# Five small edits to the order of work in a convolution and feed-forward kernel on one core

## The chip, the core and the metric

The kernel runs on one core of one Trainium2 chip. The core has a matrix engine (PE, with PEld for its weight loads), three engines for elementwise work (DVE, ACT, POOL), a queue engine (SP), and 16 DMA engines that move data between HBM and the on-chip memories. The matrix engine writes to PSUM, eight banks of 512 fp32 values per partition; everything else here lives in SBUF. The metric is device time in microseconds of one execution, and lower is better. Engines wait for each other through semaphores, and each engine works through its own instructions in the order in which the program issues them. The order is written by hand in this kernel: nothing reorders it.

## What is computed

Two layers run one after the other on x of shape 8 x 4224 x 192. The first is a causal convolution of 7 taps, with one softmax-normalised set of taps per head (8 heads of 24 channels). The second normalises each row and adds a feed-forward layer of width 768. Cut to the parts that matter:

```
out = np.einsum('hk,bskhg->bshg', softmax(weight), x_unf)       # y, the convolution
xn = (y - mean(y)) / np.sqrt(var(y) + 1e-06) * g_ln
return y + np.maximum(xn @ w_ch1, 0.0) @ w_ch2
```

All of it is fp32. The weight arrays arrive as 64-bit floats and are turned into fp32 on the chip by integer arithmetic (`split_words`, `join_low`, `join_sign`, `join_product`).

## The kernel before, in words

**Groups.** The 33,792 rows are split into 18 groups, numbered g = 0 to 17. Group 0 has 6 rows per partition, group 1 has the 8 rows per partition that are left over at the end of each of the eight sequences, group 2 has 10, and groups 3 to 17 have 16 each. For one group the work is: load x (`load_x`), convolve it into y (`first_tap` and `second_tap` on ACT, `conv` on DVE), transpose y in blocks of 32 into yt (`transpose`, DVE), multiply by the first weight (`up` or `up_mixed`), relu, multiply by the second weight (`down` or `down_fast`), transpose back (`finish_fast`), scale by the row's 1/std (`scale`, ACT) and add to the output that `store_y` has written, with an accumulating DMA (`add_to_out`, issued by POOL).

**The two big stages.** From group 3 on, both products use a recursive scheme with 7 block products in place of 8. It needs sums of quarters of the left side and of the weights. For the first product `sums_of_y` makes them, s1 = a21 + a22 and s2 = s1 - a11 on DVE and s3, s4 on POOL. `up_mixed(g)` runs seven block products over one third of the width (lines 691 to 709) and seven over the rest (712 to 761), all through `rows_of_tiles` (the matmuls are on line 533). Between them ACT copies PSUM away (line 662), DVE adds PSUM to SBUF (line 668) and POOL issues DMAs that add one SBUF tile to another (line 617). `down_fast(g)` runs the seven block products of the second weight (lines 888 to 891, 905, 906 and 909; the matmuls are on line 861). The middle ones read tiles that DVE makes with nine `half_sum` instructions (lines 897 to 899, recorded on line 828).

**What DVE does in `down_fast(g)`**, in its order: the end of the convolution of group g+1, `transpose(g + 1)` (line 893), the nine half sums, three additions to c11 (line 901), s1 and s2 of group g+1 (lines 608 and 609), a memset of one value per partition (line 612) that POOL waits for before s3, and the statistics of group g+1 (`moments`, line 448). After that come, in the next `up_mixed`, `finish_fast` (lines 923 and 925) and the convolution of group g+2 (line 417).

**What ACT does in `down_fast(g)`.** The block products copy their results with ACT (line 867), one copy for each of three chunks. Behind each copy ACT takes some items from a list, `work`, as many as `behind` says: 3 after each chunk of the first product, then 2, 2 and 3, and 2 in lines 905 and 906. The list is put together at the end of `up_mixed` (lines 790 to 793): a relu of `one.c22`, then 14 scalings of the previous group's output (the item of row 7 and the last one also issue an output DMA on POOL), and among them, behind nine items, the two relus of `two.c22` (lines 792 and 675). Then follow the 16 items of `first_tap` and `second_tap` of group g+2; the last of them issues four DMAs on POOL that add tap 1 to y (`add_second_tap`, line 409).

**The start.** PE first runs idle matmuls on no data of interest (`keep_warm`, line 367). DVE and ACT turn the first weight into fp32 in three pieces, and PE then subtracts its mean (`centre_w1`, lines 332 to 348) with matmuls on lines 335 and 340. Between those PE runs the convolution of three heads of group 0 (`conv_on_pe`, line 326); ACT copies those results into y (line 330). The other five heads of group 0 are DVE's. Then `transpose(0)` (line 1000) makes yt of group 0 in one instruction, and `up(0)` starts. Its matmuls read the six blocks of 32 channels in order, and with them six blocks of w1, the last two of which ACT copies at the very end (line 362).

**Loads.** `load_x(1)` (line 994) issues eight DMAs, one for each sequence, all on SP's queue, behind the load of the second weight into `raw2` (line 990). Where `gate` is set, a memset of one value by DVE in front of the DMA makes the DMA wait until DVE has come to that point.

Of the kernel before, what the change touches and what calls it, by code (L numbers as in the profile page):

```python
# [16 lines left out]
def kernel(  # L17
# [29 lines left out]
    nc = tc.nc  # L47
    PSUM = bass.MemoryType.PSUM
    B, S, D = x.shape
    H, K = weight.shape  # L50
    F = moe_w_ch1.shape[1]
    P = 128
# [9 lines left out]
    NC = D // C  # L62
# [23 lines left out]
    CH = NC // 2  # L86
# [46 lines left out]
    def load_x(g, queue=nc.sync, pad=True, gate=False):  # L133
        b, j0, n = groups[g]
        t = xpool.tile([P, J + PAD, D], F32, tag="xg", name=f"xg{g}")
        xg[g] = t
        flat = t.rearrange("p j d -> p (j d)")
        if gate:
            nc.vector.memset(t[0:1, 0:1, 0:1], 0.0)
        if b is None:  # L140
            for b in range(B):
                queue.dma_start(
                    out=flat[LP * b : LP * b + LP, 0 : (PAD + n) * D],
                    in_=bass.AP(
                        tensor=x.tensor, offset=(b * S + P * R - PAD) * D,
                        ap=[[n * D, LP], [1, (PAD + n) * D]],
                    ),
                )
            return
        if j0:  # L150
            queue.dma_start(
                out=flat[:, 0 : (n + PAD) * D], in_=xr[b, :, (j0 - PAD) * D : (j0 + n) * D]
            )
            return
        if b:

            queue.dma_start(
                out=flat[:, 0 : (PAD + n) * D],
                in_=bass.AP(
                    tensor=x.tensor, offset=(b * S - PAD) * D, ap=[[R * D, P], [1, (PAD + n) * D]]  # L160
                ),
            )
            if pad:
                nc.gpsimd.memset(t[0:1, 0:PAD, :], 0.0)
            return
        nc.gpsimd.memset(t[0:1, 0:PAD, :], 0.0)
        for p0, p1 in ((16, P), (1, 16)):
            nc.sync.dma_start(
                out=flat[p0:p1, 0 : (PAD + n) * D],
                in_=bass.AP(  # L170
                    tensor=x.tensor, offset=(b * S + p0 * R - PAD) * D,
                    ap=[[R * D, p1 - p0], [1, (PAD + n) * D]],
                ),
            )
        nc.sync.dma_start(out=flat[0:1, PAD * D : (PAD + n) * D], in_=xr[b, 0:1, 0 : n * D])
# [156 lines left out]
    def centre_w1():  # L332
        pm = [take_bank()[:, 0:FH] for r in range(2)]
        for r in range(2):
            nc.tensor.matmul(pm[r], share[0], w1f[:, r, :], start=True, stop=False)
            if r == 0:
                keep_warm(2)
        conv_on_pe(PE_HEADS[2])
        for r in range(2):
            nc.tensor.matmul(pm[r], share[1 + r], w1f[:, 2, :], start=False, stop=True)  # L340
        tap_matrices(PE_HEADS[1], range(3))
        for r in range(2):
            nc.scalar.copy(mean[:, FH * r : FH * r + FH], pm[r])
        tap_matrices(PE_HEADS[1], range(3, K))
        conv_on_pe(PE_HEADS[0])
        copies_of_w1(0, [(q, 0) for q in range(NQ)])
        conv_on_pe(PE_HEADS[1])
        copies_of_w1(2, [(NQ, 0), (NQ + 1, 0), (NQ, 1), (NQ + 1, 1)])
# [15 lines left out]
    def keep_warm(times):  # L364

        for _ in range(times):
            nc.tensor.matmul(idle[:, 0:P], less, less, start=True, stop=True)
# [224 lines left out]
    ysums, rows_left = {}, {}  # L592
# [5 lines left out]
            cuts = [(slice(0, J), slice(T * h, T * h + T)) for h in range(2)]  # L598
        return [yt[g][:, js, CH * k : CH * k + CH, ts] for js, ts in cuts for k in range(2)]

    def sums_of_y(g, engine):

        room = upool.tile([P, 3 * HJ * CH * C], F32, tag="ys", name=f"ysums{g}")
        room = room.rearrange("p (v j c t) -> p v j c t", v=3, c=CH, t=width(g))
        s1, s2, s3 = [room[:, v] for v in range(3)]
        a11, a12, a21, a22 = quarters_of_y(g)
        ysums[g] = s1, s2, s3, a21
        nc.vector.tensor_tensor(s1, a21, a22, op=ALU.add)
        nc.vector.tensor_tensor(s2, s1, a11, op=ALU.subtract)
        if engine is not nc.vector:  # L610

            nc.vector.memset(s3[:, 0:1, 0:1, 0:1], 0.0)
        engine.tensor_tensor(s3, a21, a11, op=ALU.subtract)
        engine.tensor_tensor(a21, a12, s2, op=ALU.subtract)
# [4 lines left out]
    def up_mixed(g, ahead, pending):  # L619
# [7 lines left out]
        a11, a12, a21, a22 = quarters_of_y(g)  # L627
        s1, s2, s3, s4 = ysums[g]
# [161 lines left out]
        work = [lambda: one.relu(one.c22)]  # L790
        work += [lambda j=j: scale_one(j) for j in range(2, done)]
        half = [lambda i=i: two.relu(two.c22[:, i : i + 1]) for i in range(PAIR)]
        return work[0:9] + half + work[9:]

    def down_row(rows, left):

# [47 lines left out]
    def down_fast(g, work):  # L844
        n = fast[g]
        t = width(g)
        w = n * T
        a = of_products(g)
        flat = cpool.tile([P, NC, NFAST * C], F32, tag="cs", name=f"cs{g}")[:, :, 0 : n * C]
        order = "p c (h j t) -> p c h j t" if t == C else "p c (j h t) -> p c h j t"  # L850
        cs = flat.rearrange(order, h=2, t=t)
        free = a[:, 1, 0].rearrange("p f q j t -> p (f q) j t")
        parts = [free[:, 0:CH], free[:, CH : 2 * CH]]
        banks = [take_bank() for c in range(CH) for i in range(2)]

        def product(bank, left, right, to, first, behind=0):
            for c in range(CH):
                dst = banks[2 * c + bank]
                for f in (PAIR, *range(PAIR)):
                    for q in range(NQ):  # L860
                        nc.tensor.matmul(  # L861
                            dst[C * q : C * q + C, 0:w], right[:, f, C * c : C * c + C],
                            left[:, f, q], start=(first and f == PAIR), stop=(f == PAIR - 1),
                            skip_group_check=True,
                        )
                if to is not None:
                    nc.scalar.copy(  # L867
                        to[:, c], dst[:, 0:w].rearrange("p (j t) -> p j t", t=t)
                    )
                for one in work[:behind]:  # L870
                    one()
                del work[:behind]

        b = quarters_of_w2()
        c11, c21 = cs[:, 0:CH, 0], cs[:, 0:CH, 1]
        c12, c22 = cs[:, CH:NC, 0], cs[:, CH:NC, 1]
        if g == 2:
            work += [lambda h=h: first_tap(4, heads=(h, h + 1)) for h in range(7, H)]
            work += [lambda h=h: second_tap(4, heads=(h, h + 1)) for h in range(H)]
        elif g + 2 < NG:  # L880
            work += [
                lambda tap=tap, h=h: tap(g + 2, heads=(h, h + 1))
                for tap in (first_tap, second_tap) for h in range(H)
            ]
        behind = (1, 1, 1, 1) if g == 2 else (3, 2, 2, 3)
        if g + 1 == NG:
            behind = (0, 0, 1, 2)
        product(0, a[:, 0, 0], b[0], c11, True, behind[0])
        product(1, a[:, 1, 0], w2sums[:, 2], c22, True, behind[1])
        product(1, a[:, 1, 1], w2sums[:, 3], c21, False, behind[2])  # L890
        product(1, a[:, 0, 1], b[2], None, True, behind[3])
        if g + 1 < NG:
            transpose(g + 1)
            if g == 2:
                b11, b12 = quarters_of_w1()[0:2]
                nc.vector.tensor_tensor(b12, b12, b11, op=ALU.subtract)
        half_sum(g, (1, 1), (1, 1), (1, 0), ALU.add)
        half_sum(g, (0, 0), (1, 1), (0, 0), ALU.add)
        half_sum(g, (0, 1), (0, 1), (1, 1), ALU.subtract)
        for c in range(CH):  # L900
            nc.vector.tensor_tensor(
                c11[:, c], c11[:, c], banks[2 * c + 1][:, 0:w].rearrange("p (j t) -> p j t", t=t),
                op=ALU.add,
            )
        product(0, a[:, 1, 1], w2sums[:, 1], parts[0], False, 2)
        product(0, a[:, 0, 0], w2sums[:, 0], parts[1], False, 2)
        for one in work:
            one()
        product(0, a[:, 0, 1], b[3], c12, False)
        if g + 1 < NG:  # L910
            sums_of_y(g + 1, nc.gpsimd)
            if g == 2:
                load_x(5, gate=True)
            moments(g + 1)
        else:
            finish_fast(g, 0, flat, cs, parts)
        return flat, cs, parts
# [73 lines left out]
        out=raw2.rearrange("p (c d) w -> p c (d w)", d=D),  # L991
        in_=w2_words.rearrange("(c p) d -> p c d", p=P),
    )
    load_x(1)
    tap_matrices(PE_HEADS[0], range(4))
    first_tap(0, heads=(0, PE_HEADS[0]))
    tap_matrices(PE_HEADS[0], range(4, K))
    conv(0, heads=(0, PE_HEADS[0]))
    centre_w1()
    transpose(0)  # L1000
    spare = cpool.tile([P, NC * NFAST * C], I32, tag="cs", name="spare")
    words_2 = (raw2, spare[:, 0 : NF * D], spare[:, NF * D : 2 * NF * D])
    split_words(*words_2, scaled=False)
# [13 lines left out]
    for g in range(NG):  # L1017
# [6 lines left out]
        else:  # L1024
            up(g)
            work = []
# [90 lines left out]
```

## Time and profile before

| | |
|---|---|
| device time, median of 3 runs | 953.44 us (951.1 to 954.62) |
| the profiled execution's own time | 953.63 us |
| span of its profile | 951.4 us |
| granted PE clock over the span | 0.999 |
| PE busy / weight loads | 944.5 us / 750.8 us |
| DVE / ACT / POOL busy | 894.1 / 700.0 / 340.8 us |

The span runs from the first to the last instruction of the profile; 2.2 us of the execution's own time lie around it. A group of instructions is named by engine, line and operation, with the tiles it writes and reads (out<-in). In the timeline the columns are start and duration in us, engine, line, operation, tiles, shapes and count; brackets hold the idle time just before and what ended it. PE's durations are modelled and overlap, so in the dense stages the time from one start to the next says more than the busy share. "issue" is idle time for which the profile shows no reason.

### The profile page before, as it was taken

How to read it: one execution, taken by the hardware profiler on the slowest of the kernel's cores; microseconds unless marked ns; L12 is line 12 of the kernel's file. 1: busy time of each engine (PE TensorE's matmuls, PEld its weight loads, DVE VectorE, ACT ScalarE, POOL GpSimd, SP SyncE). 2: the span in 40 equal slices, each digit the busy share in tenths (PEclk: the TensorE clock that was granted, in tenths of full speed). 3: DMA queues.
4: the chain of work that ended last, by engine and by line, in shares of the span. 5: the costliest groups of instructions: out<-in, count | busy, mean ns of one | idle time of the engine just before them, and what ended most of it. 6: DMA issues, size and time to landing. Idle time of an engine off the chain costs nothing.

```text
span 951.4 us, 38106 instructions
## 1 busy us (share of the span) xinstructions
PE 944.5 (99%) x16914; PEld 750.8 (79%) x16914; DVE 894.1 (94%) x1496; ACT 700.0 (74%) x1250; POOL 340.8 (36%) x474
## 2 busy tenths in 40 slices
PE   9999999999999999999999999999999999999998
PEld 7998896877859687787968778696877869586787
DVE  7999998999999999999999999999999999999867
ACT  6853678597877959787895968779696877967362
POOL 1158422723144142534218231452416332261330
PEclk9999999999999999999999999999999999999999
DMA  8359589689797887979697897979889797778261
GB/s 207 102 159 209 100 222 285 123 181 245 136 259 146 233 172 171 234 136 272 132 246 148 192 227 134 272 134 250 163 188 219 129 278 136 174 134 144 40 121 68
DMA packets 39834, 169.37 MB, mean 178 GB/s; under 512 B 4469, under 2 KB 8182, under 8 KB 33655
## 3 DMA queue, kind: packets, MB, share of 16 engines
q0 software_dynamic: 32864, 106.77, 60.5%
q1 hardware_dynamic: 6800, 60.16, 17.2%
q8 instruction: 133, 2.18, 0.9%
q14 instruction: 31, 0.25, 0.1%
q10 hardware_dynamic: 6, 0.00, 0.0%
HBM read 38.93 MB, written 50.33 MB: 94 GB/s over the span
## 4 chain that ended last, share of the span: by engine, by line
PE 67%; DVE 0%; issue 0%
PE ps L861 34%; PE ps L533 32%; PE ps L798 1%; DVE y L955 0%
## 5 line engine op out<-in xcount | busy, mean ns | idle before, releaser
L417 DVE SCALAR_TENSOR_TENSOR y<-xg,taps,y 128x384 f32<-128x384 f32 (+3 forms) x720 | 364.7, 582 | 3.3 <-DMA y<-tb 1.7
L861 PE MATMUL ps<-room,w2sums 128*32 128x256 f32 (+2 forms) x4608 | 246.9, 371 | 0.0
L533 PE MATMUL ps<-yt,w 32*128 32x256 f32 (+2 forms) x4160 | 237.9, 373 | 0.3 <-DVE yt L428 0.3
L533 PEld LDWEIGHTS ps<-yt,w 32*128 32x128 f32 x4160 | 211.0, 185 | 21.6 <-issue 6.2
L861 PEld LDWEIGHTS ps<-room,w2sums 128*32 128x32 f32 x4608 | 151.4, 110 | 89.5 <-ACT room L675 4.6
L662 ACT COPY room<-ps 128x512 f32<-128x512 f32 (+1 forms) x213 | 174.2, 859 | 62.6 <-PE ps L533 62.6
L861 PE MATMUL ps<-room,w 128*32 128x256 f32 (+2 forms) x3456 | 189.9, 371 | 0.4 <-DVE room L668 0.3
L828 DVE TENSOR_TENSOR room<-room 128x1024 f32<-128x1024 f32 (+2 forms) x147 | 161.2, 1170 | 22.4 <-PE ps L861 14.9
L861 PEld LDWEIGHTS ps<-room,w 128*32 128x32 f32 x3456 | 112.9, 110 | 69.3 <-DVE room L668 5.3
L533 PE MATMUL ps<-ysums,w1sums 32*128 32x256 f32 x2160 | 127.2, 376 | 0.3 <-issue 0.3
L533 PEld LDWEIGHTS ps<-ysums,w1sums 32*128 32x128 f32 x2160 | 116.5, 185 | 5.3 <-issue 0.7
L951 POOL DMA_DIRECT2D out_dram<-ot x69 | 59.0, 941 | 155.4 <-ACT ot L940 102.3
L409 POOL DMA_DIRECT2D y<-tb x59 | 52.5, 1386 | 154.5 <-ACT room L867 110.2
L867 ACT COPY cs<-ps 128x256 f32<-128x256 f32 (+2 forms) x192 | 70.0, 367 | 45.8 <-PE ps L861 45.8
L675 ACT ACTIVATE room<-room 128x1024 f32<-128x1024 f32 (+1 forms) x89 | 92.8, 1072 | 3.2 <-DMA room<-parts_cs 3.2
L940 ACT ACTIVATE ot<-ot,r 128x192 f32<-128x192 f32 x224 | 90.9, 464 | 0.0
L380 ACT ACTIVATE y<-xg,taps 128x384 f32<-128x384 f32 (+3 forms) x141 | 73.1, 608 | 0.4 <-DMA xg<-in_x_dram 0.4
L448 DVE BATCH_NORM_STATS2 st<-y 128x6 f32<-128x192 f32 x264 | 70.1, 344 | 0.0
L867 ACT COPY room<-ps 128x256 f32<-128x256 f32 (+2 forms) x96 | 35.5, 370 | 46.6 <-PE ps L861 44.9
L533 PE MATMUL ps<-yt,w1sums 32*128 32x256 f32 x1080 | 69.2, 375 | 0.0
L533 PE MATMUL ps<-ysums,w 32*128 32x256 f32 x1080 | 68.5, 374 | 0.0
L398 ACT ACTIVATE tb<-xg,taps 128x384 f32<-128x384 f32 (+1 forms) x120 | 66.1, 628 | 0.0
(119 smaller groups left out, 939.9 us busy)
## 6 DMA issues: line engine op xcount, KB each, us to landing
xg<-in_x_dram SPq DMA_DIRECT2D x14, 2112.0 KB, 16.2
room<-room POOLq DMA_DIRECT2D x45, 512.0 KB, 5.3
out_dram<-ot POOLq DMA_DIRECT2D x59, 384.0 KB, 9.6
y<-tb POOLq DMA_DIRECT2D x58, 384.0 KB, 8.8
out_dram<-y SPq DMA_DIRECT2D x13, 1536.0 KB, 9.1
room<-parts_cs POOLq DMA_DIRECT2D x28, 512.0 KB, 6.8
room<-parts_tb POOLq DMA_DIRECT2D x14, 1024.0 KB, 7.6
xg<-in_x_dram POOLq DMA_DIRECT2D x1, 2112.0 KB, 14.0
```

Of the source, the lines that this page charges most:

```text
L380: nc.scalar.mul(y[g][:, 0:n, cs], xg[g][:, 0:n, cs], taps[:, h, 0:1])
L398: nc.scalar.mul(tb[g][:, 0:n, cs], xg[g][:, 1 : 1 + n, cs], taps[:, h, 1:2])
L417: nc.vector.scalar_tensor_tensor(out=y[g][:, 0:n, cs], in0=t[:, k : k + n, cs], scalar=taps[:, h, k : k + 1], in1=y[g][:, 0:n, cs], op0=AL ...
L448: nc.vector.bn_stats(out=sums[g][:, j, :], in_=y[g][:, j, :])
L533: nc.tensor.matmul(banks[:, q, i * w + j1 * t : i * w + j2 * t], right[rows, c, P * i : P * i + P], left[rows, j1:j2, c, :], start=start, ...
L662: nc.scalar.activation(to, of, AF.Relu) if relu else nc.scalar.copy(to, of)
L675: nc.scalar.activation(c, c, AF.Relu)
L828: nc.vector.tensor_tensor(a[:, *dst, f], a[:, *left, f], a[:, *right, f], op=op)
L861: nc.tensor.matmul(dst[C * q : C * q + C, 0:w], right[:, f, C * c : C * c + C], left[:, f, q], start=(first and f == PAIR), stop=(f == PAI ...
L867: nc.scalar.copy(to[:, c], dst[:, 0:w].rearrange("p (j t) -> p j t", t=t))
L940: nc.scalar.mul(ots[g][:, j, :], ots[g][:, j, :], rstd[g][:, j : j + 1])
L951: nc.gpsimd.dma_start(out=rows[:, d0:d1], in_=src[:, d0:d1], accum_op=ALU.add)
```

## The change

1. `load_x(1)` is gated, with the memset over all 128 partitions, and its last four DMAs are issued by POOL (`nc.gpsimd`) and not by SP.
2. The two idle matmuls inside `centre_w1` are removed.
3. The sum s1 of group g+1 is made in a function of its own, right behind `transpose(g + 1)`, ahead of the nine half sums. s2, s3 and s4 stay where they were.
4. In the work list the two relus of `two.c22` come behind seven items and not nine, and an item that does nothing stands between them. With 3 items behind each chunk of the first product, the first relu and the empty item end the first product's share, and the second relu is the first item of the second product's share.
5. `transpose(0)` is issued as two instructions, over the first and the last three blocks of channels.

```diff
         if gate:
-            nc.vector.memset(t[0:1, 0:1, 0:1], 0.0)
+            nc.vector.memset(t[0 : 1 if b is not None else P, 0:1, 0:1], 0.0)
         if b is None:
             for b in range(B):
-                queue.dma_start(
+                (queue if b < B // 2 else nc.gpsimd).dma_start(
                     out=flat[LP * b : LP * b + LP, 0 : (PAD + n) * D],
...
             nc.tensor.matmul(pm[r], share[0], w1f[:, r, :], start=True, stop=False)
-            if r == 0:
-                keep_warm(2)
         conv_on_pe(PE_HEADS[2])
...
-    def sums_of_y(g, engine):
-
+    def first_sum_of_y(g):
         room = upool.tile([P, 3 * HJ * CH * C], F32, tag="ys", name=f"ysums{g}")
         room = room.rearrange("p (v j c t) -> p v j c t", v=3, c=CH, t=width(g))
         s1, s2, s3 = [room[:, v] for v in range(3)]
         a11, a12, a21, a22 = quarters_of_y(g)
         ysums[g] = s1, s2, s3, a21
         nc.vector.tensor_tensor(s1, a21, a22, op=ALU.add)
+
+    def sums_of_y(g, engine):
+        a11, a12, a21, a22 = quarters_of_y(g)
+        s1, s2, s3, _ = ysums[g]
         nc.vector.tensor_tensor(s2, s1, a11, op=ALU.subtract)
...
-        return work[0:9] + half + work[9:]
+        return work[0:7] + [half[0], lambda: None, half[1]] + work[7:]
...
             transpose(g + 1)
+            first_sum_of_y(g + 1)
             if g == 2:
...
-    load_x(1)
+    load_x(1, gate=True)
...
-    transpose(0)
+    transpose(0, 0, CH)
+    transpose(0, CH, NC)
```

## The prediction, made before the changed kernel was run

> **What bounds the kernel.** I read the page's busy shares and the chain that ended last, then the windows of single `down_fast` stages, then who waited for whom, then the timeline around each edit.
>
> ```profile
> PE 944.5 (99%) x16914; PEld 750.8 (79%) x16914; DVE 894.1 (94%) x1496; ACT 700.0 (74%) x1250; POOL 340.8 (36%) x474
> PE ps L861 34%; PE ps L533 32%; PE ps L798 1%; DVE y L955 0%
> ```
>
> PE is busy all along and alone makes the chain from 312.6 us to the end. The pieces of that chain are nearly constant: 27.6 us for an `up_mixed`, 27.4 for a `down_fast`. So work taken from DVE, ACT or a queue is worth nothing by itself; only a stall of PE, or work that PE does itself, can be won. PE's busy time hides short stalls, so I compared whole stages. These are the windows of two `down_fast` (the columns are the window, its length, then the busy times, the clock, the DMA share and GB/s):
>
> ```profile
> 312.63:339.96 27.33, 27.33 (x504) 16.32 (x504) 26.25 (x38) 22.52 (x51) 9.35 (x10) 1.00 0.96 245
> 367.58:395.00 27.42, 27.42 (x507) 16.17 (x505) 26.23 (x38) 22.72 (x51) 9.35 (x10) 1.00 0.96 247
> ```
>
> They do the same work, and the second is 0.09 us longer. The waits of PE's weight loads in these two windows show why: the second has a wait of 0.4 us for ACT's relu on L675, and the first has none. Over the run:
>
> ```profile
> PEld ps L861 <- ACT room L675: 4.6, 13, 0.4
> PE ps L861 <- DVE room L668: 0.3, 1, 0.3
> ```
>
> **The relus (edit 4).** The third block product of `down_fast` reads the relued c22. ACT's timeline, in the group whose stage starts at 422.61, shows the relus late:
>
> ```profile
> 427.70 0.37 ACT L867 COPY cs<-ps 128x256 f32<-128x256 f32 x1
> 427.96 1.16 ACT L940 ACTIVATE ot<-ot,r 128x192 f32<-128x192 f32 x3
> 429.01 0.37 ACT L867 COPY cs<-ps 128x256 f32<-128x256 f32 x1
> 429.26 2.02 ACT L675 ACTIVATE room<-room 128x1024 f32<-128x1024 f32 x2
> 431.16 0.37 ACT L867 COPY cs<-ps 128x256 f32<-128x256 f32 x1
> ```
>
> ACT works without a pause here. A scaling takes it (429.01 - 427.96)/3 = 0.35 us, a copy 0.26 from start to start, a relu 0.96. Product three starts when two products of 3.9 us are over, at 430.4. Its first 8 of 24 matmuls per chunk read `one.c22`, the next 8 the first relu's block, and the third 8 the second relu's, at 430.4 + 16 x 0.053 = 431.28. The second relu ends at 431.28: just too late. After the change ACT does copy 427.70, one scaling at 427.96, the first relu at 428.31, the copy at 429.27, the second relu at 429.53, ending at about 430.6. That is 0.7 us sooner, so this wait goes. The copy at 429.01 moves to 429.27 and ends at 429.64; it frees the bank that product three writes from 430.4 on, so it is not late. Everything behind comes 0.3 us sooner, since two scalings move back behind it and the empty item leaves one out.
>
> Each wait is worth between nothing and the load's whole wait, 4.6/13 = 0.35 us. The two windows give 0.09 (loads run ahead of the matmuls, so most of a load's wait is covered), and I take that: 13 x 0.09 = **-1.2 us**, with ends 0 and -4.6. What comes next on PE is the change from one form of matmul to another at the ends of a stage, which this doesn't touch.
>
> The empty item also moves the last `second_tap` item behind one more item, so its four DMAs on POOL (L409) are issued one step of ACT later, 66.1/120 = 0.55 us. Behind them on POOL stand s3 and s4. They start at 447.59 now, and PE reads s3 only in the fourth product of the next stage, 450.49 + 3 x 1.3 = 454.4; s3 and s4 take 1.82 us each, so 0.55 us is hidden. For the DMAs' reader see the rivals.
>
> **The first sum (edit 3).**
>
> ```profile
> 429.86 3.38 DVE L428 STREAM_TRANSPOSE yt<-y 128x3072 f32<-128x3072 f32 x1
> 434.25 10.31 DVE L828 TENSOR_TENSOR room<-room 128x1024 f32<-128x1024 f32 x9 [1.02 <-PE ps L861]
> 445.48 0.95 DVE L608 TENSOR_TENSOR ysums<-yt 128x768 f32<-128x768 f32 x1
> ```
>
> Behind the transpose DVE sits idle for 1.02 us, because the first half sum overwrites what product three reads. By the groups table this idle time is 14.1 us in 14 stages, 1.0 each. The sum takes 0.95, so it fits, with at most 0.05 us left over. PE needs the third half sum at 438.26, and it ends at 434.25 + 3 x 1.15 = 437.7, so 0.5 us of cover remains; without it the sum would cost 0.95 a group. Behind the half sums DVE then runs 0.95 us ahead, through s2, the statistics and `finish_fast`, until the convolution (L417), which must wait for the taps of L409. DVE's next meeting with PE is L668, where DVE already waits for PE (10.8 us in 16). Being early there buys nothing. I take **0**, with ends +0.05 x 14 = +0.7 and -0.3 (the one stall of PE behind L668, shown above).
>
> **The start (edits 2 and 5).**
>
> ```profile
> 12.60 0.81 PE L335 MATMUL ps<-room 128*128 128x384 f32 x2
> 13.24 0.61 PE L367 MATMUL ps<-room 128*128 128x128 f32 x4
> 13.69 0.81 PE L335 MATMUL ps<-room 128*128 128x384 f32 x2
> 22.98 1.38 DVE L428 STREAM_TRANSPOSE yt<-y 128x1152 f32<-128x1152 f32 x1 [1.74 <-ACT y L330]
> 23.31 0.82 PE L357 MATMUL ps<-room 32*128 32x384 f32 x8
> 24.41 4.18 PE L533 MATMUL ps<-yt,w 32*128 32x192 f32 x96 [0.28 <-DVE yt L428]
> ```
>
> PE runs from matmul to matmul from 7.74 to 24.1. The four idle matmul records hold it from 13.24 to 13.69, **0.45 us**, and what follows has its data (the last piece of w1f ends at 12.55). All of PE's chain, and ACT's copies that hang on it, come 0.45 sooner. The transpose waits 1.74 us for ACT's copy of the last head, then takes 1.38. In halves, the first fits into that idle time, and the second takes about 0.78 by the rows of 768 (0.98) and 1152 columns (1.38). It ends at 22.98 - 0.45 + 0.78 = 23.3 instead of 24.36. PE is through with L357 at 23.7, so its idle 0.28 us before L533 goes too. But ACT sets the pace behind that: four copies of w1, a relu of raw words, an eviction, four first taps and an eviction, without a pause from 24.15 to 29.6, where PE's third block of `up(0)` (29.71) waits for it. This chain starts when PE ends L357, so it moves by 0.45 only. I take **-0.45** for both edits; ends 0 and -0.73. From there PE is dense to the end, so what is won at 29.71 stays.
>
> **The load of group 1 (edit 1).**
>
> ```profile
> 11.45 6.72 SPq L142 DMA_DIRECT2D xg<-in_x_dram  x8
> 27.42 1.49 ACT L380 ACTIVATE y<-xg,taps 128x192 f32<-128x192 f32 x4
> ```
>
> The gate holds all eight until DVE ends the last `join_product` at 12.55, so they start 1.2 us later. The memset (0.06 us) falls into DVE's wait of 0.17 us before 12.72. Behind the waiting DMAs on SP stands `store_y(0)`, which goes at 22.97 anyway, and on POOL nothing until 45.1. POOL's four issues take 0.9 to 1.4 us each, 3.6 to 5.5 in all. The median landing of these pieces is 7.9 us, so they are there by 18.1 + 7.9 = 26.0 at the latest of these, and ACT reads them at 27.0. I take **0**; the upper end is a rival.
>
> During this load the DMA engines are already occupied: their share is 1.17, 0.94 and 1.08 in the windows from 16 to 22 us. The Trainium skill speaks against this edit: "DMA: Bandwidth & Descriptors", section "Queues, rings and completion order", says that each DMA engine takes turns between the queues that have work, so POOL's half would no longer stand behind the second weight but slow it down. By that rule the weight comes later; its reader is DVE's L233, which starts at 24.28 with no wait for a DMA, so the sum stays the same by rule and by row.
>
> **Sum.** -1.2 - 0.45 = -1.65 us against the profiled execution's own 953.63 (0.2 above the median): **952.0 us**.
>
> **Rivals.**
> - *The relus were not it* (0.2): another operand is late by the same 0.09 us, or the transition between stages shifts. Only the start's gain is left: 953.63 - 0.45 = 953.2. For it: the short stalls marked "issue" come and go between equal stages. Against it: the stage without this wait is the shorter one.
> - *More is won* (0.14): PE keeps the 0.28 us at the start, and the stall behind L668 goes: 953.63 - 1.2 - 0.73 - 0.3 = 951.4. If each relu wait were worth 0.35, it would be 948.3 (0.04 of this).
> - *Taps late, slower* (0.12): L409's DMAs land 0.55 us later while DVE wants them 0.95 sooner. In one group DVE waited 1.37 us for them now, and PE lost 0.3. The wait costs PE time once the landing is over 0.5 us past the convolution's present start, since DVE waits 0.5 us for PE at L668. The four are issued from 443.63 to 447.17; with the median landing of 8.8 the last is there by 456.0, and the convolution starts at 457.1: 1.1 us of margin. If half of the 13 groups passed that point by 0.55, it would be +3.6 - 1.65 = 955.6.
> - *x(1) late, slower* (0.04): if POOL's pieces took the 16.2 us of the big loads, they would land at 34, 7 us past ACT's need: up to 953.63 - 1.65 + 7 = 959. It costs from a landing at 27.0 on.
>
> The forecast itself has 0.5. About 0.5% (4.8 us) is what a measurement of this kernel can tell from no change: faster than that 0.04, slower 0.07, within it 0.89. The range runs from 951.4 to 955.6, widened below by the spread of equal runs (951.1 to 954.6): 950.2 to 955.4.
>
> **What would show it.** After: no wait of PE's loads for L675, and `down_fast` windows of 27.33; the half sums still start about 11.65 us into the stage; L335 back to back; the first L533 at about 23.7 and the third block of `up(0)` at about 29.3; no DMA wait in front of L380. Wrong: a wait for L828 in PE's fifth product, more waits of L417 for y<-tb with L668 late behind them, or stages still at 27.42.

## The result and the profile after

The changed kernel took 950.55 us (median of 22 runs, 949.12 to 952.52), and the kernel before took 951.99 us in 22 runs on the same chip (950.66 to 954.62). The ratio is 0.9983, with a 95% interval of 0.9977 to 0.9990: 1.6 us less (0.0017 x 952), between 1.0 and 2.2. That is a real gain, and it lies inside the half per cent named in the prediction. The profiled execution took 951.32 us itself, with a span of 949.4.

The page shows a PE just as busy as before:

```profile
PE 942.7 (99%) x16910; PEld 754.5 (79%) x16910; DVE 898.4 (95%) x1498; ACT 700.2 (74%) x1250; POOL 344.3 (36%) x478
```

**The relus.** No wait of PE's loads for the relu is left; before there were 13. These are the windows of two `down_fast`, the second in the same group as the 27.42 us of before:

```profile
311.49:338.82 27.33, 27.33 (x507) 16.27 (x505) 27.16 (x42) 22.71 (x51) 9.72 (x10) 1.00 0.96 245
366.43:393.76 27.33, 27.33 (x506) 16.36 (x504) 27.16 (x42) 22.72 (x51) 9.71 (x10) 1.00 0.95 244
```

Twelve of the 14 stages of groups 3 to 16 now last 27.33 us. ACT's timeline in the second of these stages shows why:

```profile
371.52 0.37 ACT L868 COPY cs<-ps 128x256 f32<-128x256 f32 x1
371.78 0.47 ACT L942 ACTIVATE ot<-ot,r 128x192 f32<-128x192 f32 x1
372.14 1.05 ACT L676 ACTIVATE room<-room 128x1024 f32<-128x1024 f32 x1
373.08 0.37 ACT L868 COPY cs<-ps 128x256 f32<-128x256 f32 x1
373.34 1.08 ACT L676 ACTIVATE room<-room 128x1024 f32<-128x1024 f32 x1
```

The second relu ends at 374.42, 7.99 us into the stage. Before, it ended 8.67 us into it: 0.68 sooner, where 0.7 was forecast. The copy between the relus comes 6.65 us into the stage (6.66 forecast).

**The moved sum.** DVE's timeline of the same stage:

```profile
373.67 3.38 DVE L426 STREAM_TRANSPOSE yt<-y 128x3072 f32<-128x3072 f32 x1
377.08 0.96 DVE L605 TENSOR_TENSOR ysums<-yt 128x768 f32<-128x768 f32 x1
377.98 10.31 DVE L829 TENSOR_TENSOR room<-room 128x1024 f32<-128x1024 f32 x9
```

The sum fills the idle time to within a few hundredths of a microsecond, and the half sums start 11.55 us into the stage (11.64 before, when PE was later). DVE's waits for PE ahead of the half sums, 14.9 us in 14 stages before, are gone. Some 6 us of that reappear as waits at DVE's next meeting with PE, L669 (10.8 us before; the first two lines below):

```profile
DVE room L669 <- PE ps L531: 14.1, 14, 2.3
DVE room L669 <- ACT room L676: 3.0, 2, 1.8
DVE y L415 <- DMA y<-tb: 1.9, 4, 0.7
```

Another 4.3 us went into `finish_fast`, which in 12 stages now begins while POOL still makes s4 (this line is the group of its additions; before, the same 28 instructions took 929 ns each, 26.0 us in all).

```profile
L925 DVE TENSOR_TENSOR cs<-cs,room 128x768 f32<-128x768 f32 x28 | 30.3, 1082 | 0.0
```

Most of the rest is the shorter span and the convolution's own waits (L415, 4.9 us for 3.3).

**The start.** PE from the first weight's matmuls to the third block of `up(0)`:

```profile
7.74 5.48 PE L365 MATMUL ps<-room 128*128 128x128 f32 x28
13.06 1.46 PE L335 MATMUL ps<-room 128*128 128x384 f32 x4
...
23.97 4.09 PE L531 MATMUL ps<-yt,w 32*128 32x192 f32 x96
...
29.68 1.58 PE L531 MATMUL ps<-yt,w 32*128 32x192 f32 x32 [0.33 <-ACT room L521]
```

The L335 matmuls are back to back, and PE no longer waits for the transpose. But the third block starts at 29.68, and before it started at 29.71. In these two executions the start won nothing, because the 28 idle matmuls ahead of L335 ended 0.46 us later than before. This is their line in the profile before:

```profile
7.74 5.02 PE L367 MATMUL ps<-room 128*128 128x128 f32 x28
```

The experiments show that PE's pace steps up at another moment in every profile, with the same instructions ahead of it, so this is not the change's doing.

The two spans differ by 2.0 us. Thirteen waits of 0.09 make 1.2 of it. Another 1.0 is short stalls of PE that go by no stage: before, three `down_fast` stages (27.93, 27.88 and 27.82 us) carried them, after, two did (27.63 and 27.43), and the `up_mixed` stages add up to the same 415.26 us in both. The tail behind the last stage gives 0.2 back (12.2 us, before 12.0).

### The profile page after: what moved, and what is told of

Its sections match the earlier page's. It is cut to its first block, busy times and chain, and to the rows that moved or that the text cites. A ratio compares the mean times of both kernels' runs of the same rounds, so it can differ in the third digit from the quotient of the medians.

```text
span 949.4 us, 38094 instructions
## 1 busy us (share of the span) xinstructions
PE 942.7 (99%) x16910; PEld 754.5 (79%) x16910; DVE 898.4 (95%) x1498; ACT 700.2 (74%) x1250; POOL 344.3 (36%) x478
## 4 chain that ended last, share of the span: by engine, by line
PE 99%; ACT 1%; DMA 0%; issue 0%; DVE 0%; ACTq 0%
PE ps L531 48%; PE ps L862 44%; PE ps L799 4%; PE ps L365 1%; PE ps L326 1%; PE ps L352 0%; ACT room L521 0%; ACT w L360 0%; ACT y L378 0%; PE ps L355 0%; PE ps L335 0%; PE ps L338 0%; DMA room<-in_weight_dram 0%; PE ps L973 0%; PE ps L211 0%
## 5 line engine op out<-in xcount | busy, mean ns | idle before, releaser
L415 DVE SCALAR_TENSOR_TENSOR y<-xg,taps,y 128x384 f32<-128x384 f32 (+3 forms) x720 | 364.6, 581 | 4.9 <-DMA y<-tb 1.9
L862 PEld LDWEIGHTS ps<-room,w2sums 128*32 128x32 f32 x4608 | 154.7, 110 | 84.7 <-issue 0.6
L942 ACT ACTIVATE ot<-ot,r 128x192 f32<-128x192 f32 x224 | 94.7, 468 | 0.0
L378 ACT ACTIVATE y<-xg,taps 128x384 f32<-128x384 f32 (+3 forms) x141 | 73.1, 607 | 0.6 <-DMA xg<-in_x_dram 0.6
```

The lines of the kernel that those rows point to most:

```text
L378: nc.scalar.mul(y[g][:, 0:n, cs], xg[g][:, 0:n, cs], taps[:, h, 0:1])
L415: nc.vector.scalar_tensor_tensor(out=y[g][:, 0:n, cs], in0=t[:, k : k + n, cs], scalar=taps[:, h, k : k + 1], in1=y[g][:, 0:n, cs], op0=AL ...
L862: nc.tensor.matmul(dst[C * q : C * q + C, 0:w], right[:, f, C * c : C * c + C], left[:, f, q], start=(first and f == PAIR), stop=(f == PAI ...
L942: nc.scalar.mul(ots[g][:, j, :], ots[g][:, j, :], rstd[g][:, j : j + 1])
```

## The experiments

All ratios are against the kernel before, run on the same chip in the same session. The changed kernel's is 0.9983. Their intervals reach 0.001 to 0.002, or 1 to 2 us, to either side, so the terms of the prediction are read from the stages of the profiles, and the times only confirm their sum.

**e1_relus_only**: the kernel before, with this edit alone.

```diff
-        return work[0:9] + half + work[9:]
+        return work[0:7] + [half[0], lambda: None, half[1]] + work[7:]
```

> The kernel before with edit 4 alone (relus around a copy). Theory A (the relu wait is worth 0.09 us in each of some 13 stages): no wait of PE's loads for the relu of L675, down_fast windows of 27.33 us instead of 27.42, and 1.2 us less than before (ratio about 0.9987). Rival B (the relus were not it, the gain comes from DVE running ahead after the moved sum): windows stay at 27.42 and the time is that of before, ratio 1.000.

951.55 us, ratio 0.9990 (0.9981 to 1.0000). All 14 stages last 27.33 us, and there is no wait for the relu. Theory A holds: 14 x 0.09 = 1.26 us.

**e2_no_relus**: the changed kernel with that edit undone.

```diff
-        return work[0:7] + [half[0], lambda: None, half[1]] + work[7:]
+        return work[0:9] + half + work[9:]
```

> The changed kernel with edit 4 undone. Theory A: the 13 or so waits for the relu are back at about 0.35 us of the loads each, windows at 27.42, and of the gain only the start is left: 0.3 to 0.5 us less than before (ratio about 0.9996). Rival B: nearly the whole gain stays, ratio 0.9983.

952.29 us, ratio 0.9998 (0.9990 to 1.0007). Thirteen of the 14 stages last 27.42 to 27.44 us (the other 27.82), and the waits of PE's loads are back:

```profile
PEld ps L862 <- ACT room L676: 5.1, 14, 0.4
```

So edits 1, 2, 3 and 5 together are worth too little for this number of runs to show, and the relus are the larger part. The rival "the relus were not it" is out.

**e3_no_empty_item**: is the place around the copy needed?

```diff
-        return work[0:7] + [half[0], lambda: None, half[1]] + work[7:]
+        return work[0:7] + half + work[7:]
```

> The changed kernel without the empty item, so that both relus come ahead of the first copy of the second product. Theory A: that copy starts at about 7.7 us into the stage and not at 6.7, ends at about 8.1, and holds the bank that product three writes from 7.8 on: PE waits 0.3 to 0.4 us for L868 in each of 14 stages, 4 to 6 us slower than the changed kernel. Rival (the place around the copy is not needed, only the earlier relus are): windows stay at 27.33, same time as the changed kernel.

954.03 us, ratio 1.0017 (1.0004 to 1.0031): 3.2 us over the changed kernel. Most stages last 27.58 to 27.61 us, 0.26 more than 27.33, and PE's loads wait for the copy:

```profile
PEld ps L862 <- ACT cs L868: 7.6, 14, 0.8
```

14 x 0.26 = 3.6. The mechanism is the one expected, a copy that holds the bank of product three; its price is 0.26 a stage and not 0.3 to 0.4. The loads wait 0.54 each and cover half of it.

**e4_relus_late**: the relus two items later than in the kernel before.

```diff
-        return work[0:7] + [half[0], lambda: None, half[1]] + work[7:]
+        return work[0:11] + half + work[11:]
```

> The changed kernel with the two relus behind eleven items, two scalings later than in the kernel before. Theory A: both relus then stand behind the copy of the second chunk of product two, the second ends about 1.0 us later than in the kernel before, and PE, which was only just late there, now waits for nearly all of it: 0.9 to 1.0 us in each of 14 stages, 12 to 15 us slower than the changed kernel, windows of 28.2 to 28.4. Rival (loads run ahead and cover most of a wait): windows below 27.6, at most 4 us.

964.05 us, ratio 1.0123 (1.0110 to 1.0137): 13.3 us over the changed kernel. Thirteen stages last 28.38 us or more, 1.05 over 27.33. The wait shows on PE itself now, where the kernel before had it on the loads alone:

```profile
PEld ps L862 <- ACT room L676: 21.7, 28, 1.3
PE ps L862 <- ACT room L676: 8.7, 26, 0.8
```

So 1 us more of lateness costs 1 us in each stage, and only the first 0.3 us is cheap: the kernel before stood just on the edge.

**e5_sum_twice**: s1 computed twice in its new place.

```diff
-        nc.vector.tensor_tensor(s1, a21, a22, op=ALU.add)
+        for _ in range(2):
+            nc.vector.tensor_tensor(s1, a21, a22, op=ALU.add)
```

> The changed kernel with the moved sum s1 computed twice in its place (the second overwrites the first with the same values). Theory A: behind the transpose DVE has 1.0 us of idle time and PE leaves 0.5 us of cover at its fifth product; one sum of 0.95 fits, two pass the cover by 0.4 to 0.5 us: PE waits 0.4 to 0.5 us for the half sums in 14 stages, 6 to 7 us slower than the changed kernel, windows of about 27.8. Rival (half sums have more cover than that, since the first matmuls of a chunk read other blocks): windows 27.33 and the same time.

957.64 us, ratio 1.0058 (1.0037 to 1.0078): 7.1 us over the changed kernel. The stages last 27.85 to 27.88 us, 0.53 over 27.33, or 7.4 in 14, and PE waits for the half sums:

```profile
PEld ps L863 <- DVE room L830: 11.5, 15, 0.8
```

One sum is free and a second costs over half of its time: 0.4 us of cover was left, where the prediction had 0.5.

**e6_close_in_halves**: is PE's gap behind each `up_mixed` DVE's doing? The profile names DVE's L668 (here L672) as the releaser, 15 times.

```diff
-                    nc.vector.tensor_tensor(c, c, self.seen(banks), op=ALU.add)
+                    src = self.seen(banks)
+                    for qs in (slice(0, 2), slice(2, NQ)):
+                        to = c[:, :, qs]
+                        nc.vector.tensor_tensor(to, to, src[:, :, qs], op=ALU.add)
```

> The changed kernel with DVE's addition on L669 (PSUM to SBUF, 2.29 us, at the end of up_mixed) issued in two halves of two banks each, so that the first banks are free 1.1 us sooner. If PE's 0.25 us at the change from up_mixed to down_fast is a wait for this addition, each of 14 groups is 0.15 to 0.25 us shorter: 2 to 3.5 us less than the changed kernel. If it is the change of the matmuls' form, the time stays within 0.5 us and the gap of about 0.30 us from the last start of one stage to the first of the next stays.

949.75 us, ratio 0.9974 (0.9965 to 0.9983), not distinguishable from the changed kernel. The gap stays at 0.30 to 0.31 us, at a point where the first half has been done for over a microsecond:

```profile
363.36 2.35 DVE L672 TENSOR_TENSOR room<-room,ps 128x1024 f32<-128x1024 f32 x2 [0.95 <-PE ps L531]
...
365.96 2.10 PEld L865 LDWEIGHTS ps<-room,w 128*32 128x32 f32 x44 [0.33 <-DVE room L672]
```

DVE's second half ends 0.25 us before PE goes on, and in the changed kernel the whole addition ends 0.12 us before; the gap is the same. So the named releaser is a coincidence in time, and what is left is the change of the matmuls' form, from rows of 32 to columns of 32, which no run here takes away. The Trainium skill's "TensorEngine Tiling (Array Packing)", section "Key Properties", states that changing the tiling mode drains the engine; it gives no figure, and this case agrees with one, 0.30 us from the last start to the first against 0.05 to 0.06 inside a stage. The opposite change, from `down_fast` to `up_mixed`, shows 0.31.

**e7_more_idle**: eight idle matmuls where the kernel before had two.

```diff
             nc.tensor.matmul(pm[r], share[0], w1f[:, r, :], start=True, stop=False)
+            if r == 0:
+                keep_warm(8)
```

> The changed kernel with eight idle matmuls in the place where the kernel before had two. Theory A: PE's chain at the start is dense, so they add 16 x 0.11 = 1.8 us to the start of up(0), and PE is dense to the end, so 1.8 us stay: 1.8 us slower than the changed kernel, 0.3 to 0.5 slower than before. Rival (the start waits for DMAs or ACT, and PE has idle time there or later that takes it up): less than 0.5 us slower.

953.53 us, ratio 1.0007 (0.9994 to 1.0019): 2.3 us over the changed kernel. Its profile has the same clock history at the start as the changed kernel's (first L335 at 13.12 and 13.06), and the third block of `up(0)` starts at 31.52 against 29.68: 1.84 us later, as expected. PE is dense behind it, and the time agrees within its interval.

**e8_one_queue**: edit 1 undone (all of x(1) on SP, no gate).

```diff
-                (queue if b < B // 2 else nc.gpsimd).dma_start(
+                queue.dma_start(
...
-    load_x(1, gate=True)
+    load_x(1)
```

> The changed kernel with edit 1 undone: all of x(1) on SP, without a gate. Theory A: the reader of x(1) does not wait with or without it, so the same time as the changed kernel within 0.5 us; x(1) starts 1.2 us or more sooner. Rival (the gate lets x(0) and the weights land sooner): ACT's first tap waits longer for x(0) than in the changed kernel, and the start is later by that, up to 0.7 us.

950.67 us, ratio 0.9976 (0.9966 to 0.9986). No loss from undoing it, within the interval. The gate does not bring x(0) sooner: ACT's first tap on it starts at 12.81 here and at 12.83 in e6, and over all profiles at 11.5 to 12.8 without the gate and at 11.7 to 13.1 with it.

**The clock at the start.** e8's profile shows the second thing that decides the start. These are PE's lines to compare with those of the changed kernel above:

```profile
7.24 3.39 PE L365 MATMUL ps<-room 128*128 128x128 f32 x28
10.46 1.65 PE L335 MATMUL ps<-room 128*128 128x384 f32 x4
12.88 1.34 PE L326 MATMUL ps<-xg,room 128*128 128x144 f32 x9 [0.77 <-DMA xg<-in_x_dram]
```

The same 28 idle matmuls take 3.39 us here and 5.48 there. In the trace their starts lie 213 ns apart at first and 112 ns later, and the step comes between 5.4 and 7.6 us in eight of the 14 profiles of this study ("early" below) and between 11.1 and 12.4 in the other six ("late"), which include both kernels'. The granted clock in the profile says 1.00 throughout, so that this is PE's clock is read from the pace alone. The Trainium skill's "TensorE: Matmul & The Clock Gate", section "Part 1: The HAM clock gate (the "warmup" mystery)", tells of half speed until a free-running window of about 3.4 us has been busy, and that the moment differs from run to run. The ratio of 1.9 agrees. The early steps come 3.4 to 5.5 us after PE's first matmul (2.1 us) and the late ones 9.0 to 10.2, a far wider spread than the half microsecond that the section gives.

Where the step is early, the loads can come too late. In five of the eight early profiles (e3, e4, e6, e8, e12) PE waits 0.3 to 0.8 us for x(0) behind L335, so fewer matmuls ahead of it buy nothing there. And ACT comes early to x(1). In all 14 profiles the third block of `up(0)` starts 2.2 to 2.3 us after ACT's first tap of group 1 (L378, before L380). In five of the early ones ACT stood idle for 0.25 to 0.85 us ahead of that tap (e4, e5, e6, e9, e12). This is e5's:

```profile
25.95 1.49 ACT L378 ACTIVATE y<-xg,taps 128x192 f32<-128x192 f32 x4 [0.61 <-issue]
```

The profile names x(1) in e6 and e12 and nothing in e4, e5 and e9. But the semaphore records in the traces, which tell when each piece of x(1) landed, put the last landing 0.1 to 0.25 us ahead of the tap in all five. In e1 and e8 it lies 0.15 us ahead of the tap, too, without a wait of ACT, and of the early ones only e3 has time to spare (1.0 us).

Two more kernels test what matmuls at the start are worth, and one tests the margin of x(1).

**e11_idle_back**: e8 with the two idle matmuls back.

```diff
             nc.tensor.matmul(pm[r], share[0], w1f[:, r, :], start=True, stop=False)
+            if r == 0:
+                keep_warm(2)
```

> The changed kernel with edits 1 and 2 undone: x(1) on SP alone without a gate, and the two idle matmuls back. Theory: if PE comes early to full speed, PE waits for x(0) right behind the second L335 with or without them, so the first L326 starts when x(0) has landed and up(0) starts as in e8_one_queue; if it comes late, all of PE's chain is 0.45 us later than without them. Over many runs 0 to 0.45 us more than e8_one_queue, too little for these rounds to tell. Rival (the 0.45 us counts in every execution): the first L326 starts 0.4 us or more after x(0) has landed, also where PE is early at full speed.

951.27 us, ratio 0.9995 (0.9982 to 1.0007): 1.8 us over e8 by the ratios, more than expected, but the two intervals leave from nearly nothing to 4 us. The profile caught a late step, at the same moment as in the changed kernel's profile:

```profile
13.06 0.81 PE L335 MATMUL ps<-room 128*128 128x384 f32 x2
13.71 0.61 PE L367 MATMUL ps<-room 128*128 128x128 f32 x4
14.15 0.81 PE L335 MATMUL ps<-room 128*128 128x384 f32 x2
```

With L335 at 13.06 in both, the third block starts at 30.12 here and at 29.68 in the changed kernel. So the matmuls are worth 0.44 us where the step is late. For the early case there is e1 (idle matmuls kept). Its PE starts L326 at 12.08, 0.46 us after ACT's first tap on x(0) (11.62), where PE follows that tap by 0.06 or 0.07 us in the profiles in which it waits for x(0). So the idle matmuls can hold PE up there as well, the sign that the rival names. But the third block could not have come much sooner: x(1) had landed at 25.45, and ACT's tap of group 1 started at 25.59. It starts at 27.87, and in e3 and e4 (early, without the matmuls) at 27.85 and 27.94. In these profiles they are worth nothing that shows.

**e9_less_idle**: e8 with fewer idle matmuls in the stretch ahead.

```diff
-    keep_warm(14)
+    keep_warm(8)
```

> The changed kernel with edit 1 undone (x(1) on SP alone, no gate) and with 8 idle matmuls instead of 14 in the second stretch ahead of the first weight's matmuls. Theory: what the start costs depends on when PE comes to full speed (matmul starts 213 ns apart before, 112 after; between 7 and 12 us in the profiles so far). Where it comes late, the idle matmuls hold the first L335 back to 12.6 to 13.1, and 12 fewer records let it start by 11.2, so that the third block of up(0) comes 0.5 to 1.4 us sooner; where it comes early, the landing of x(0) sets the pace and nothing changes. Over many runs 0.2 to 0.8 us less than e8_one_queue, ratio 0.997 to 0.9975, and the spread of runs narrower. Rival: PE needs the idle matmuls to come to full speed, and with fewer it comes later: same time or up to 1 us more.

949.40 us, ratio 0.9975 (0.9965 to 0.9985), the same as e8, where 0.2 to 0.8 us less was expected. The step was early in this profile, and the first L335 waits for DVE:

```profile
9.11 0.88 PE L335 MATMUL ps<-room 128*128 128x384 f32 x2 [0.33 <-DVE room L266]
10.61 0.91 PE L335 MATMUL ps<-room 128*128 128x384 f32 x2 [0.62 <-DVE raw L991]
```

The step came at 5.5 us, before the shortened stretch begins (6.73), and so it did in e12 (6.4 and 7.17). So neither profile tells whether these idle matmuls bring PE to full speed. The case for which the edit was made, a late step, was not caught, so what it is worth stays open.

**e10_x1_on_pool**: all of x(1) on POOL.

```diff
-                (queue if b < B // 2 else nc.gpsimd).dma_start(
+                nc.gpsimd.dma_start(
```

> The changed kernel with all eight DMAs of x(1) on POOL, still behind the gate. Theory (x(1) has little margin behind the gate): eight issues end at about 17, the last lands 10 to 11.8 us later at 27 to 29, ACT's first tap of group 1 waits 0.5 to 2 us for it, the third block of up(0) comes as much later, and the time is 0.5 to 2 us over the changed kernel. Rival (a first tap has 2 us or more to spare): no DMA wait of ACT at 26 to 28 us, and the time of the changed kernel.

949.06 us, ratio 0.9977 (0.9968 to 0.9986). The theory did not come true: the pieces landed 6.8 us after their issue (median; 8.1 at most), by 24.1, and ACT did not wait. But this profile has a late step, and ACT's tap started only at 27.21; in e12, with the same loads and an early step, ACT waited. The single pieces took longer to land where both queues share them: by the semaphore records their median is 9.3 to 10.7 us in the seven profiles with both, 7.9 to 8.8 in the five with SP alone, and 6.9 and 8.6 with POOL alone. The eight together did not: from the first issue to the last landing it was 11.9 to 14.6, 13.2 to 14.5, and 11.6 and 13.2 us. On SP alone the eighth piece is issued late, 6.2 to 6.8 us after the first, within 0.02 us of the landing of the second weight in all five profiles; the two share a semaphore. So no way of issuing x(1) is shown to bring it sooner.

**e12_pool_less_idle**: e10 and the edit of e9 together.

```diff
-                (queue if b < B // 2 else nc.gpsimd).dma_start(
+                nc.gpsimd.dma_start(
...
-    keep_warm(14)
+    keep_warm(8)
```

> The changed kernel with all of x(1) on POOL and 8 idle matmuls instead of 14 ahead of the first weight's matmuls, to join the two edits of the start that looked best. If PE comes late to full speed in this profile, the first L335 starts by 11.2 and not at 13, and the third block of up(0) by 28.7 and not at 29.5; if early, the first L335 starts at about 9.1 and the third block at 27.6 to 28. Over many runs 2 to 3 us under the kernel before (ratio 0.997 to 0.998), 0.3 to 1 us under the changed kernel. Rival: the idle matmuls bring PE to full speed and fewer make it late: the time of the changed kernel or more.

949.74 us, ratio 0.9972 (0.9954 to 0.9990). The step was early again. The first L335 came at 9.67 and the third block at 28.55, later than the 9.1 and the 27.6 to 28 expected: x(0) held PE for 0.61 us, and x(1), whose last piece landed at 26.21, held ACT for 0.35. e8, e9, e10 and e12 all have a lower ratio than the changed kernel's 0.9983, with overlapping intervals: none of them is shown to beat it.

## Why the prediction was right, point by point

The forecast was 1.65 us less than before, and the measured ratio is 1.6 us less. That the two agree to 0.05 us is luck, since the interval runs from 1.0 to 2.2, and the relus' term is well shown but the start's is not the same in every execution. The absolute time came out 1.45 us under the forecast of 952.0, inside the range, mostly because the forecast started from one execution of 953.63, and the median of the kernel before over 22 runs is 951.99. The range as stated ends at 955.4, a little below the 955.6 that it is said to run to; nothing here hangs on that.

- **The relus, -1.2 us.** Right in mechanism and in size. The wait is gone, every stage without a chance stall lasts 27.33 us, and 14 stages at 0.09 make 1.26 (e1, e2). Comparing two stages that do the same work, one with the wait and one without, gave the price; the load's own wait of 0.35 us would have given four times as much. The stage without the wait (312.63) was an odd one, which the prediction does not say: PE had come to it 0.34 us late, behind DVE's L668, so ACT had the time, and its second relu ended 8.36 us into the stage and not 8.67. That its length was the right measure even so is shown by e1, where 14 stages have it. The warning about the copy was right too: e3 pays 0.26 us a stage where the relus are as early but both stand ahead of the copy.
- **The empty item's late taps.** Issued at the same 21.0 us into the stage as before, and not 0.55 later, so the rival "taps late" never began. The step that failed is the count of slots as if they were time. ACT has no pause from the relus to that item, so the item ends when all the work ahead of it is done, and an empty item adds no work (e3, without it, also issues at 21.0); the copies in between came sooner (the first copy of L905's product at 18.0 us into the stage, before at 18.5). DVE waited for the taps four times instead of twice, 1.9 us in all (1.7 before), because it came sooner.
- **The sum, 0.** Right. e5 measures the cover: 0.5 us was forecast, and the second 0.95 us costs 0.53, so it is 0.4. Being early brought DVE nothing, as said; it waits at L669 for PE instead.
- **The start, -0.45 us.** Right where PE's pace steps up late (0.44, e11 against the changed kernel). Where it steps up early, what failed is "this chain starts when PE ends L357, so it moves by 0.45": ACT's chain then also waits for x(1), by 0.25 to 0.85 us in e4, e5, e6, e9 and e12, and PE for x(0), so less work on PE shows as little or nothing. So over many executions the term must be smaller than forecast; by how much, no run shows. The prediction took the start of one profiled execution for fixed; across the profiles the third block of `up(0)` starts anywhere from 27.6 to 30.1 us (e7 with its added matmuls aside), on average at 28.2 with an early step and at 29.7 with a late one. That PE's earlier start of `up(0)` buys nothing beyond ACT's chain was right: in the changed kernel it starts 5.71 us ahead of the third block, before 5.30.
- **The load of group 1, 0.** Right for the profile of the changed kernel, and there partly by luck, because two sizes were off in opposite ways. POOL's four issues took 2.2 us and not 3.6 to 5.5, and the pieces took up to 10.7 us to land and not 7.9 (12.6 in e2); the last landed at 25.4, with 26.0 forecast, and ACT read them at 27.4. With an early step ACT comes sooner, and then the wait that the rival "x(1) late" named is there. In e6, which has this edit, it is 0.85 us:

```profile
27.03 1.49 ACT L378 ACTIVATE y<-xg,taps 128x192 f32<-128x192 f32 x4 [0.85 <-DMA xg<-in_x_dram]
```

  The third block started at 29.26 there, and at 28.29 in e8, which has x(1) on one queue and a like clock history. So a late x(1) can cost about 1 us in an execution. Whether the edit makes it later is not shown, since e9 and e12 waited without it, and no run shows a gain from it. The rule of the skill that was weighed against it, turns between the queues, would slow the second weight; by the semaphore records its load took 6.7 us in the changed kernel and 6.9 before, and DVE's first read of it waited for no DMA, so no cost of that kind shows.

Still open are the short stalls in single stages, 0.1 to 0.8 us each: they stand in different stages in nearly every profile, and no experiment here touched them. Between the two main profiles they make 1.0 us, not much less than the whole change.

## What to carry to other kernels

In a kernel whose bound engine is never idle by the profile, compare equal stages: a difference of 0.09 us in 27.4, with one named wait in only one of them, is worth more than any busy share. Ask also why the other stage is without the wait. A move of work on a covered engine is free up to its cover and costs nearly its full length beyond, so work out the cover from the reader's start and not from the idle time alone. A small gain at the start of a kernel should be read from several profiles, since the start depends on when the matrix engine's pace steps up and on when the first loads land.

## What the runs showed of the hardware that was not expected

- Idle matmuls of the same kernel took 3.39 us or 5.48 us for 28, as PE's step from 213 to 112 ns between starts came before 7.6 us or after 11.1, while the profile's clock column read 1.00 in both.
- Eight loads of 168 KB landed one by one in a median of 6.9 and 8.6 us from POOL alone, 7.9 to 8.8 from SP alone, and 9.3 to 10.7 from both, but all eight together took 11.6 and 13.2, 13.2 to 14.5, and 11.9 to 14.6 us. On SP alone the eighth was issued only when the second weight, which uses the same semaphore, had landed.
- DVE's addition of 128 x 768 values takes 1.31 us instead of 0.94 where its first 0.5 us lie beside POOL's `tensor_tensor` (394.25 to 395.55 us in the changed kernel's profile, POOL until 394.74), and 1.21 where it is 0.4 us (e2). The statistics on DVE, which ran beside POOL's sums in both kernels, kept their 0.34 us. So of the 0.95 us that the moved sum brought forward, a third went to running beside another engine.
- At a change of the matmuls' form PE loses 0.25 us (0.30 from start to start, 0.05 inside a stage) in either direction, from group 3 on in every stage without another wait. From `up_mixed` to `down_fast` the profile puts it down to DVE, which had ended just before.
